# A linear-attention and highway-layer kernel rebuilt as a hand-ordered pipeline, with casting transfers and work on GpSimd

## The chip, the core and the metric

The kernel runs on one core of a Trainium2 chip. A core has TensorE (PE, matrix products into PSUM), VectorE (DVE) and ScalarE (ACT), which read PSUM and SBUF, GpSimd (POOL), which reaches SBUF only, and SyncE (SP), which starts transfers. Sixteen DMA engines carry what SP and POOL start. The metric is the device time of one execution in microseconds (us), the median of some runs; lower is better.

## What is computed

Inputs are q, k, v of shape (4 batches, 8 heads, 768 positions, 64), one decay `lam` per head, and the weights of a highway layer. First comes causal attention without softmax, in which the weight of position j for position i decays as `lam**(i-j)`:

```python
intra = np.einsum('bhic,bhjc->bhij', qb, kb) * Dmask[None]
intra = np.einsum('bhij,bhjd->bhid', intra, vb)
inter = np.einsum('bhid,bhde->bhie', qb * lam_pow[None], kv_state)
out[:, :, sl] = intra + inter
kb_dec = kb * rev_pow[None]
kv_state = lam_block[None, :, None, None] * kv_state + np.einsum('bhsd,bhse->bhde', kb_dec, vb)
```

The heads are then laid side by side, which gives x of 3072 rows and 512 columns, and the layer follows:

```python
H = np.maximum(x @ w_h, 0.0)
T = 1.0 / (1.0 + np.exp(-(x @ w_t + b_t)))
return (T * H + (1.0 - T) * x).astype(np.float32)
```

## The kernel before

The work is cut into 24 chunks: 4 batches (loop at L89) of 6 blocks of 128 positions (loop at L94). A framework places the semaphores, and its scheduler sets each engine's order from the order in which the chunks are written and from what is ready; most tiles have two buffers, PSUM tiles one. Each engine runs its own list in order.

For each chunk SP loads q, k and v for all heads as float32 (`qf`, `kf`, `vf`, L99 to L101, 256 KB each, in pieces of 256 B). DVE multiplies q by `lam**i` (`qs`, L106), v by `lam**-j` (`vb`, L107) and k by `lam**128` (`kb2`, L110; the trace shows it as `kb` too); ACT copies k to bfloat16 (`kb`, L108). PE transposes q and k head by head (L115, L116, 16 products with an identity), and ACT moves the results to SBUF (`qsT` L119, `kbT` L120). Eight products per chunk give the scores (`at_ps`, L132, contraction over 64 rows), and DVE masks them with a triangle in two halves (L133). Then three kinds of product per head: scores by v (L139, contraction over 128 rows, 64 columns), q by the state (L140, contraction over 64 rows, 64 columns) into the same PSUM tile `oa_ps`, and k by v for the next state (`kv2_ps`, L141). DVE copies the attention output to bfloat16 (`x_sbuf`, L143) and updates the state in SBUF with two operations (L145, L146).

The layer needs x transposed: PE does that (L150), ACT moves it (`x_T`, L152), and PE multiplies by the two weights (L156, L162: 4 products each of 512 columns) and adds the bias with a product over one row (L163). ACT applies Relu (L158) and Sigmoid (L165), DVE combines with three operations (L168, L170, L172), and SP stores 256 KB (L174). The weights are loaded as float32 once and cast by ACT (L75 to L79). POOL makes constants at the start and nothing else.

Of the kernel before, what the change touches and what calls it, by code (L numbers as in the profile page):

```python
# [15 lines left out]
def kernel(  # L17
# [24 lines left out]
    tri_mask = singles.tile([128, 1, 128], F32)
    make_upper_triangular(nc, tri_mask[:, 0, :], val=1.0, diag=True)

    lam_bcast = singles.tile([128, H], F32)
    nc.sync.dma_start(out=lam_bcast, in_=lam.partition_broadcast(128))
    ln_lam = singles.tile([128, H], F32)
    nc.scalar.activation(ln_lam, lam_bcast, AF.Ln)
    pow_q = singles.tile([128, H, 1], F32)
    pow_v = singles.tile([128, H, 1], F32)  # L50
    iota_i = work.tile([128, 1], mybir.dt.int32, tag="iota_i")
    nc.gpsimd.iota(iota_i, pattern=[[0, 1]], base=0, channel_multiplier=1)
    iota_f = work.tile([128, 1], F32, tag="iota_f")
    nc.vector.tensor_copy(iota_f, iota_i)
    pln = work.tile([128, H], F32, tag="pln")
    nc.vector.tensor_scalar(pln, in0=ln_lam, scalar1=iota_f, scalar2=None, op0=ALU.mult)
    nc.scalar.activation(pow_q[:, :, 0], pln, AF.Exp)
    nc.vector.reciprocal(pow_v[:, :, 0], pow_q[:, :, 0])
    lam128 = singles.tile([128, H, 1], F32)
    nc.scalar.activation(lam128[:, :, 0], ln_lam, AF.Exp, scale=float(BLK))  # L60
    iota2 = work.tile([128, 128], mybir.dt.int32, tag="iota2")
    nc.gpsimd.iota(iota2, pattern=[[1, 128]], channel_multiplier=0)
    iota2f = work.tile([128, 128], F32, tag="iota2f")
    nc.vector.tensor_copy(iota2f, iota2)
    pln2 = work.tile([128, H, 128], F32, tag="pln2")
    nc.vector.tensor_tensor(pln2, in0=ln_lam[:, :, None].to_broadcast([128, H, 128]),
                            in1=iota2f[:, None, :].to_broadcast([128, H, 128]), op=ALU.mult)
    pow_qT = singles.tile([128, H, 128], F32)
    nc.scalar.activation(pow_qT, pln2, AF.Exp)

    wh = singles.tile([128, KC, d_model], BF16)
    wt = singles.tile([128, KC, d_model], BF16)
    for kc in range(KC):
        tmp = work.tile([128, d_model], F32, tag="wtmp")
        nc.sync.dma_start(out=tmp, in_=moe_w_h[kc * 128:(kc + 1) * 128, :])  # L75
        nc.scalar.activation(wh[:, kc, :], tmp, AF.Copy)
        tmp2 = work.tile([128, d_model], F32, tag="wtmp")
        nc.sync.dma_start(out=tmp2, in_=moe_w_t[kc * 128:(kc + 1) * 128, :])
        nc.scalar.activation(wt[:, kc, :], tmp2, AF.Copy)  # L79
# [125 lines left out]
```

## Time and profile before

| | us |
|---|---|
| median of 3 runs | 248.27 (245.8 to 249.95) |
| span of the profiled execution, first to last instruction | 246.7 |
| PE busy | 209.4 (85%) |
| DVE busy | 155.8 (63%) |
| ACT busy | 111.9 (45%) |
| POOL busy | 1.4 (1%) |
| DMA queue of SP, share of 16 engines | 46.7% |

The profiled execution has no time of its own beside its span; the median of the runs is 1.6 us more than that span. An engine's busy time is the time in which it worked on an instruction; PE's ends are modelled, and matmuls overlap, so the spacing of their starts says more than their length. The chain of work goes back from the last instruction to what released it, step by step. The slices cut the span into 40 equal parts of 6.2 us; PEclk is the granted TensorE clock in tenths of 2.4 GHz, whose two levels are 1.2 and 2.4 GHz.

### The profile page before, as it was taken

The numbers are of one execution on the slowest core, as the hardware profiler recorded it, in microseconds if no ns is written. First come the engines' busy times: TensorE is split into PE (matmuls) and PEld (weight loads), VectorE is DVE, ScalarE is ACT, GpSimd is POOL, SyncE is SP. The second block draws the span as 40 slices with busy tenths as digits, with TensorE's granted clock in tenths as the row PEclk, the third lists the DMA queues.
The fourth block names the chain that finished last, engine by engine and source line by source line (L and its number), as shares of the span: only waits on it lengthen the run. The fifth ranks groups of instructions, "written<-read, shape, count | busy, mean of one in ns | idle before, by whom it ended". The sixth has DMA issues, their size and how long they took to land.

```text
span 246.7 us, 3751 instructions
## 1 busy us (share of the span) xinstructions
PE 209.4 (85%) x1464; PEld 118.4 (48%) x1464; DVE 155.8 (63%) x275; ACT 111.9 (45%) x159; POOL 1.4 (1%) x10
## 2 busy tenths in 40 slices
PE   0158988989898898998998999999979997989972
PEld 0145535455364653645554645645545563654430
DVE  1645675746675767666577667857885775885532
ACT  5664744342634545515544445544543525551210
POOL 2000000000000000000000000000000000000000
PEclk9999979558776987766777769777997576997755
DMA  5699173651754737444453743745355553110111
GB/s 130 198 264 175 45 170 101 115 128 43 170 123 94 170 88 171 115 101 103 110 128 91 166 89 86 169 88 128 86 130 130 141 128 72 43 45 1 43 43 43
DMA packets 79651, 27.51 MB, mean 111 GB/s; under 512 B 75537, under 2 KB 75537, under 8 KB 79634
## 3 DMA queue, kind: packets, MB, share of 16 engines
q1 hardware_dynamic: 79634, 27.28, 46.7%
q8 instruction: 11, 0.18, 0.3%
q14 instruction: 6, 0.05, 0.1%
HBM read 20.98 MB, written 6.29 MB: 111 GB/s over the span
## 4 chain that ended last, share of the span: by engine, by line
PE 76%; ACT 9%; DVE 7%; DMA 4%; issue 2%; SPq 0%; ACTq 0%; DVEq 0%
PE h_ps L156 16%; PE t_ps L162 14%; PE oa_ps L139 10%; PE oa_ps L140 10%; PE qT_ps L115 6%; PE kT_ps L116 5%; PE at_ps L132 5%; DVE x_sbuf L143 5%; ACT x_T L152 4%; PE t_ps L163 4%; PE xps L150 4%; PE kv_ps L141 3%; DMA vf<-in_v_dram 1%; DMA tmp<-in_moe_w_h_dram 1%; ACT kbT L120 1%
## 5 line engine op out<-in xcount | busy, mean ns | idle before, releaser
L156 PE MATMUL h_ps<-wh,x_T 128*128 128x512 bf16 x96 | 40.7, 572 | 4.8 <-ACT x_T L152 4.4
L139 PE MATMUL oa_ps<-vb,masked 128*128 128x64 bf16 x192 | 39.7, 207 | 0.5 <-DVE masked L133 0.4
L140 PE MATMUL oa_ps<-kv,qsT 64*128 64x64 bf16 x192 | 39.1, 204 | 0.0
L133 DVE TENSOR_TENSOR masked<-at_ps,tri_mask 128x512 bf16<-128x512 f32 x48 | 32.8, 683 | 8.9 <-PE at_ps L132 8.7
L162 PE MATMUL t_ps<-wt,x_T 128*128 128x512 bf16 x96 | 38.3, 543 | 0.0
L119 ACT ACTIVATE qsT<-qT_ps 64x1024 bf16<-64x1024 bf16 x24 | 24.4, 1016 | 29.1 <-PE qT_ps L115 22.2
L143 DVE CAST x_sbuf<-oa_ps 128x512 bf16<-128x512 f32 x24 | 16.6, 692 | 28.7 <-PE oa_ps L140 28.7
L115 PE MATMUL qT_ps<-id,qs 128*64 128x128 bf16 x192 | 23.2, 243 | 12.6 <-DVE qs L106 11.6
L158 ACT ACTIVATE h_sb<-h_ps 128x512 bf16<-128x512 f32 x24 | 14.3, 597 | 37.4 <-PE h_ps L156 37.4
L120 ACT ACTIVATE kbT<-kT_ps 64x1024 bf16<-64x1024 bf16 x24 | 24.2, 1010 | 13.0 <-PE kT_ps L116 13.0
L168 DVE TENSOR_TENSOR hmx<-h_sb,x_sbuf 128x512 bf16<-128x512 bf16 x24 | 10.2, 423 | 27.0 <-ACT h_sb L158 26.9
L165 ACT ACTIVATE t_sb<-t_ps 128x512 bf16<-128x512 f32 x24 | 14.3, 597 | 27.2 <-PE t_ps L163 26.1
L116 PE MATMUL kT_ps<-id,kb 128*64 128x128 bf16 x192 | 25.3, 256 | 0.3 <-ACT kb L108 0.3
L115 PEld LDWEIGHTS <-qs 128*64 128x64 bf16 x192 | 18.0, 123 | 14.0 <-DVE qs L106 11.6
L139 PEld LDWEIGHTS <-masked 128*128 128x128 bf16 x192 | 18.5, 97 | 11.5 <-issue 0.7
L162 PEld LDWEIGHTS <-x_T 128*128 128x128 bf16 x96 | 13.1, 137 | 22.7 <-issue 20.1
L132 PE MATMUL at_ps<-qsT,kbT 64*128 64x128 bf16 x192 | 21.6, 238 | 2.2 <-ACT kbT L120 1.3
L140 PEld LDWEIGHTS <-qsT 64*128 64x128 bf16 x192 | 18.0, 94 | 8.2
L152 ACT ACTIVATE x_T<-xps 128x512 bf16<-128x512 bf16 x24 | 14.2, 592 | 16.7 <-PE xps L150 16.7
L116 PEld LDWEIGHTS <-kb 128*64 128x64 bf16 x192 | 19.8, 132 | 1.8 <-ACT kb L108 0.6
L150 PE MATMUL xps<-id,x_sbuf 128*128 128x128 bf16 x96 | 12.3, 268 | 9.0 <-DVE x_sbuf L143 9.0
L145 DVE TENSOR_TENSOR kv2t<-kv,lam 64x512 bf16<-64x512 bf16 x24 | 16.2, 673 | 5.1 <-ACT lam L60 5.1
(41 smaller groups left out, 191.8 us busy)
## 6 DMA issues: line engine op xcount, KB each, us to landing
qf<-in_q_dram SPq DMA_DIRECT2D x24, 256.0 KB, 3.6
kf<-in_k_dram SPq DMA_DIRECT2D x24, 256.0 KB, 3.7
vf<-in_v_dram SPq DMA_DIRECT2D x24, 256.0 KB, 3.4
out_dram<-o_sb SPq DMA_DIRECT2D x24, 256.0 KB, 2.2
tmp<-in_moe_w_h_dram SPq DMA_DIRECT2D x4, 256.0 KB, 3.4
tmp<-in_moe_w_t_dram SPq DMA_DIRECT2D x4, 256.0 KB, 3.2
lam_bcast<-in_lam_dram SPq DMA_DIRECT2D x1, 4.0 KB, 2.9
bt_f<-in_moe_b_t_dram SPq DMA_DIRECT2D x1, 2.0 KB
```

The source lines that it names most:

```text
L115: nc.tensor.transpose(qT_ps[:, h, :], qs[:, h, :], id128)
L116: nc.tensor.transpose(kT_ps[:, h, :], kb[:, h, :], id128)
L119: nc.scalar.activation(qsT, qT_ps, AF.Copy)
L120: nc.scalar.activation(kbT, kT_ps, AF.Copy)
L132: nc.tensor.matmul(at_ps[:, hh, :], lhsT=kbT_h(h), rhs=qsT_h(h), start=True, stop=True)
L133: nc.vector.tensor_tensor(masked[:, g * (H // 2):(g + 1) * (H // 2), :], in0=at_ps, in1=tri_mask.to_broadcast([128, H // 2, BLK]), op=ALU. ...
L139: nc.tensor.matmul(oa_ps[:, h, :], lhsT=masked[:, h, :], rhs=vb[:, h, :], start=True, stop=False)
L140: nc.tensor.matmul(oa_ps[:, h, :], lhsT=qsT_h(h), rhs=kv2_h(h), start=False, stop=True)
L143: nc.vector.tensor_copy(x_sbuf, oa_ps)
L152: nc.scalar.activation(x_T, xps, AF.Copy)
L156: nc.tensor.matmul(h_ps, lhsT=x_T[:, kc, :], rhs=wh[:, kc, :], start=(kc == 0), stop=(kc == KC - 1))
L162: nc.tensor.matmul(t_ps, lhsT=x_T[:, kc, :], rhs=wt[:, kc, :], start=(kc == 0), stop=False)
```

## The change

The kernel is written anew, with the framework's scheduler off (`manual_schedule`), so that each engine's list is the order in the source.

- **Loads.** q and k (L53, L58) and the weights (L98, L99) are loaded by POOL, which casts them to bfloat16 on the way: per batch 8 transfers of 192 KB for q (96 partitions of 8 positions each) and 6 of 256 KB for k. v stays float32 on SP: per chunk in batch 0, else 1.57 MB in one transfer (L64). Batches 0 and 1 are loaded ahead of the loop, batches 2 and 3 at the end of passes 5 and 11.
- **Scaling.** q and k are not scaled. v is scaled by POOL (L165) with powers that run over the whole batch, and the output by `lam**i` where it leaves PSUM (L191).
- **Transposes.** Two heads at a time, 128 columns in one product: 4 for k per chunk (L158), 32 for q per batch (L150), in one shared PSUM tile `tr`.
- **Attention output.** It is made transposed, `o_ps` of 128 rows (two heads) and 4 x 128 columns: 4 products with a block-diagonal state (L184) and 8 with v as the stationary operand (L188). x in rows is made from it by 4 products with an identity (L209).
- **State.** It stays in PSUM and is added to by 4 products per chunk (L200); ACT copies its diagonal blocks to SBUF (L204, two copies).
- **Layer.** Relu and the subtraction are one DVE operation (L216); POOL does the last addition (L230). The bias is a product over 128 rows, of which two hold the bias.
- **Order.** Pass i of the loop does: first half of the layer for chunk i-1, scores for i+1, attention and state for i, second half of the layer for i-1, transpose of k for i+2.

```diff
...
+    ctx.enter_context(tc.manual_schedule())
...
+            nc.gpsimd.dma_start(out=qb[b][:, :, h, :], in_=q[b, h].rearrange("(p j) d -> p j d", j=J))
...
+        nc.gpsimd.dma_start(out=kb[b][:, c], in_=k[b, :, c * C:(c + 1) * C, :].rearrange("h p d -> p h d"))
...
+    nc.gpsimd.dma_start(out=wh, in_=moe_w_h.rearrange("(kc p) n -> p kc n", p=128))
+    nc.gpsimd.dma_start(out=wt, in_=moe_w_t.rearrange("(kc p) n -> p kc n", p=128))
...
-            nc.vector.tensor_tensor(qs, in0=qf, in1=pow_q.to_broadcast([128, H, D]), op=ALU.mult)
-            nc.vector.tensor_tensor(vb, in0=vf, in1=pow_v.to_broadcast([128, H, D]), op=ALU.mult)
-            nc.scalar.activation(kb, kf, AF.Copy)
...
-                nc.tensor.matmul(oa_ps[:, h, :], lhsT=masked[:, h, :], rhs=vb[:, h, :], start=True, stop=False)
-                nc.tensor.matmul(oa_ps[:, h, :], lhsT=qsT_h(h), rhs=kv2_h(h), start=False, stop=True)
...
+        tr = ps.tile([128, J, QP], BF16, tag="tr", name="tr")
+        for j in range(J):
+            nc.tensor.transpose(tr[:, j, :], qb[b][:, j, 2 * hp:2 * hp + 2, :], id128[0:QP, 0:QP])
+        nc.scalar.activation(qT[b][:, hp].rearrange("p c (q j) -> p (c q) j", j=J),
+                             tr.rearrange("p j q -> p q j"), AF.Copy)
...
+        nc.gpsimd.tensor_tensor(vs[n], in0=vf[b][:, :, c, :], in1=pow_k[:, :, c, :].to_broadcast([C, H, D]), op=ALU.mult)
...
+                nc.tensor.matmul(o_ps[n][:, hp, :], lhsT=s_bd[n % 2][:, hp, :], rhs=qT[b][:, hp, c, :],
+                                 start=(hp == 0), stop=False, skip_group_check=True)
...
+                nc.tensor.matmul(o_ps[n][64 * e:64 * e + 64, hp, :], lhsT=vs[n][:, 2 * hp + e, :], rhs=masked[n][:, e, hp, :],
...
+        nc.vector.tensor_tensor(xT[n], in0=o_ps[n], in1=pow_q[:, :, c * C:(c + 1) * C], op=ALU.mult)
...
+            nc.tensor.matmul(kv_ps[b][:, hp, :], lhsT=kb[b][:, c, 2 * hp:2 * hp + 2, :], rhs=vs[n][:, 2 * hp:2 * hp + 2, :],
...
+        nc.vector.scalar_tensor_tensor(hmx[n], in0=h_ps, scalar=0.0, in1=x_sb[n], op0=ALU.max, op1=ALU.subtract)
...
+        nc.gpsimd.tensor_tensor(o_sb, in0=thmx, in1=x_sb[n], op=ALU.add)
...
+    for i in range(N + 1):
+        if i >= 1:
+            ffn_xh(i - 1)
+        if i + 1 < N:
+            scores(i + 1)
+            scale_v(i + 1)
+        if i < N:
+            attn(i)
+            state(i)
+        b, c = divmod(i, NCH)
+        if c < NP and b + 1 < B:
+            trans_q(b + 1, c)
+        if i >= 1:
+            ffn_t(i - 1)
+            combine(i - 1)
+        if i + 2 < N:
+            trans_k(i + 2)
+        if c == NCH - 1 and b + 2 < B:
+            load_v(b + 2)
+            for c in range(NCH):
+                load_k(b + 2, c)
+            load_q(b + 2)
...
```

Three places in the engines' lists. The names in brackets are semaphores: `DMASW0` to `DMASW7` are eight lanes that POOL's transfers take in turn, and a transfer that names a lane waits until the one eight before it has landed. The first place is POOL's list at the start of the program, before, where it makes constants:

```order
masks.py:197 MEMSET id_64 128x128
masks.py:65 MEMSET tri_mask 128x128
masks.py:199 ISA
masks.py:199 AFFINE_SELECT id_64<-id_64 128x128 [waits Pool_49]
masks.py:66 AFFINE_SELECT tri_mask<-tri_mask 128x128 [waits Pool_49]
L52 IOTA iota_i 128x1
L62 IOTA iota_90 128x128
```

And the same place now, without the lanes, where `qb_76`, `kb_74` and `vf_85` belong to batch 0, `qb_118` and `kb_127` to batch 1:

```order
L94 IOTA tq_i 128x768
L58 DMA kb_74<-in_k_dram 128x8x64
L98 DMA wh<-in_moe_w_h_dram 128x4x512
L99 DMA wt<-in_moe_w_t_dram 128x4x512
L58 DMA kb_74<-in_k_dram 128x8x64 x4
L53 DMA qb_118<-in_q_dram 96x8x64 x8
L58 DMA kb_127<-in_k_dram 128x8x64 x6
L165 TENSOR_TENSOR vs<-vf_85,pow_k 128x512 x3
L230 TENSOR_TENSOR o_sb<-thmx,x_sb 128x512
```

The transfers of both batches and of the weights, 30 with the 9 that stand ahead of these rows, come before the first scaling of v. The second place is POOL's list at the end of pass 5, now (before, POOL has nothing there); `kb_661` and `qb_668` belong to batch 2:

```order
L165 TENSOR_TENSOR vs<-vf_134,pow_k 128x512 [waits DMAHW3_49,PE_49,Pool_49]
L230 TENSOR_TENSOR o_sb<-thmx,x_sb 128x512 [waits DMAHW5_49,DVE_49]
L58 DMA kb_661<-in_k_dram 128x8x64 [waits DMASW6_49,PE_49]
L58 DMA kb_661<-in_k_dram 128x8x64 [waits DMASW7_49]
L58 DMA kb_661<-in_k_dram 128x8x64 [waits DMASW0_49]
L58 DMA kb_661<-in_k_dram 128x8x64 [waits DMASW1_49]
L58 DMA kb_661<-in_k_dram 128x8x64 [waits DMASW2_49]
L58 DMA kb_661<-in_k_dram 128x8x64 [waits DMASW3_49]
L53 DMA qb_668<-in_q_dram 96x8x64 [waits DMASW4_49]
L53 DMA qb_668<-in_q_dram 96x8x64 [waits DMASW5_49]
L53 DMA qb_668<-in_q_dram 96x8x64 [waits DMASW6_49]
```

Five more transfers of q follow before the next scaling of v, that of chunk 7. The third place is PE's list in pass 6, now, where the transposes of q for batch 2 begin:

```order
L200 LDWEIGHTS kb_127
L200 MATMUL kv_ps<-vs,kb_127 128x128
L150 LDWEIGHTS qb_668 [waits DMASW5_49,DMASW4_49]
L150 MATMUL tr<-id_91,qb_668 128x96 [waits PE_49]
L150 LDWEIGHTS qb_668
```

They wait for the first two transfers of q, the 7th and 8th of the 14 that POOL starts at the end of pass 5. Before, the same work on PE, the transposes of a chunk's q and k, stands among the products of the chunk ahead, and what it needs comes from DVE and ACT:

```order
L140 LDWEIGHTS qsT
L140 MATMUL oa_ps<-kv_786,qsT 128x64
L141 LDWEIGHTS kb_1236
L141 MATMUL kv_ps<-vb,kb_1236 64x64
L115 LDWEIGHTS qs
L115 MATMUL qT_ps<-id_64,qs 64x128
```

So the loads of a batch, which were spread over its six chunks, now stand in one block, and PE's list meets the transfers themselves.

## Rows read from the trace of the kernel before

**Rows 1.** Page, part 1: busy time, share of the span, instructions.

```profile
PE 209.4 (85%) x1464; PEld 118.4 (48%) x1464; DVE 155.8 (63%) x275; ACT 111.9 (45%) x159; POOL 1.4 (1%) x10
```

**Rows 2.** Page, part 2: 40 slices, busy tenths and granted clock.

```profile
PE   0158988989898898998998999999979997989972
PEclk9999979558776987766777769777997576997755
```

**Rows 3.** Page, part 4: chain that ended last, by engine, then by line.

```profile
PE 76%; ACT 9%; DVE 7%; DMA 4%; issue 2%; SPq 0%; ACTq 0%; DVEq 0%
PE h_ps L156 16%; PE t_ps L162 14%; PE oa_ps L139 10%; PE oa_ps L140 10%; PE qT_ps L115 6%; PE kT_ps L116 5%; PE at_ps L132 5%; DVE x_sbuf L143 5%; ACT x_T L152 4%; PE t_ps L163 4%; PE xps L150 4%; PE kv_ps L141 3%; DMA vf<-in_v_dram 1%; DMA tmp<-in_moe_w_h_dram 1%; ACT kbT L120 1%
```

**Rows 4.** Timeline, PE, 172 to 178 us: start, length, operation, count.

```profile
172.36 0.20 PE L139 MATMUL oa_ps<-vb,masked 128*128 128x64 bf16 x1
172.50 0.20 PE L140 MATMUL oa_ps<-kv,qsT 64*128 64x64 bf16 x1
172.63 0.20 PE L139 MATMUL oa_ps<-vb,masked 128*128 128x64 bf16 x1
...
173.43 0.63 PE L115 MATMUL qT_ps<-id,qs 128*64 128x128 bf16 x8
...
177.08 1.04 PE L156 MATMUL h_ps<-wh,x_T 128*128 128x512 bf16 x4 [0.17 <-ACT x_T L152]
177.96 1.03 PE L162 MATMUL t_ps<-wt,x_T 128*128 128x512 bf16 x4
```

**Rows 5.** Timeline, PE, 159 to 169 us, the same operations at wider spacing.

```profile
159.79 1.89 PE L156 MATMUL h_ps<-wh,x_T 128*128 128x512 bf16 x4
161.47 1.91 PE L162 MATMUL t_ps<-wt,x_T 128*128 128x512 bf16 x4
...
167.02 1.06 PE L116 MATMUL kT_ps<-id,kb 128*64 128x128 bf16 x8
```

**Rows 6.** Windows: us, busy of PE, PEld, DVE, ACT, POOL, granted clock, DMA share, GB/s.

```profile
175.92:184.20 8.28, 6.68 (x59) 4.02 (x59) 7.48 (x14) 3.93 (x7) 0.00 (x0) 0.99 0.40 101
105.00:106.00 1.00, 1.00 (x5) 0.41 (x4) 1.00 (x3) 0.00 (x0) 0.00 (x0) 0.50 0.36 63
```

**Rows 7.** Groups by line: shapes, count; busy, mean ns; idle before.

```profile
L133 DVE TENSOR_TENSOR masked<-at_ps,tri_mask 128x512 bf16<-128x512 f32 x48 | 32.8, 683 | 8.9 <-PE at_ps L132 8.7
L107 DVE TENSOR_TENSOR vb<-vf,pow_v 128x512 bf16<-128x512 f32 x24 | 16.3, 677 | 2.5 <-DMA vf<-in_v_dram 2.5
L170 DVE TENSOR_TENSOR thmx<-t_sb,hmx 128x512 bf16<-128x512 bf16 x24 | 10.1, 422 | 13.0 <-ACT t_sb L165 12.9
L119 ACT ACTIVATE qsT<-qT_ps 64x1024 bf16<-64x1024 bf16 x24 | 24.4, 1016 | 29.1 <-PE qT_ps L115 22.2 <-PE oa_ps L140 5.0 <-PE at_ps L132 1.4
L165 ACT ACTIVATE t_sb<-t_ps 128x512 bf16<-128x512 f32 x24 | 14.3, 597 | 27.2 <-PE t_ps L163 26.1 <-DVE vb L107 1.1
L60 ACT ACTIVATE lam<-ln_lam 128x8 f32<-128x8 f32 x1 | 0.2, 209 | 0.0
masks.py:66 POOL TENSOR_SCALAR_AFFINE_SELECT tri_mask<-tri_mask 128x128 f32<-128x128 f32 x1 | 0.3, 293 | 0.0
```

**Rows 8.** Windows, columns as in rows 6: three stretches with 256 KB loads.

```profile
93.00:94.00 1.00, 0.48 (x6) 0.27 (x6) 0.70 (x2) 1.00 (x2) 0.00 (x0) 1.00 0.94 278
94.00:95.00 1.00, 0.77 (x12) 0.63 (x12) 1.00 (x2) 0.83 (x3) 0.00 (x0) 1.00 1.07 243
95.00:96.00 1.00, 0.91 (x5) 0.40 (x4) 1.00 (x3) 0.59 (x2) 0.00 (x0) 0.68 1.20 251
```

**Rows 9.** Transfers: SP's issues in the timeline, then time to landing.

```profile
11.02 0.43 SPq L101 DMA_DIRECT2D vf<-in_v_dram  x1
15.58 1.88 SPq L99 DMA_DIRECT2D qf<-in_q_dram  x1
...
qf<-in_q_dram SPq DMA_DIRECT2D x24, 256.0 KB, 3.6
out_dram<-o_sb SPq DMA_DIRECT2D x24, 256.0 KB, 2.2
```

More of the change, by code (lines that the diff above doesn't have):

```diff
@@ L40 @@
+    nc.sync.dma_start(out=bt_f[32:33, :], in_=moe_b_t.partition_broadcast(1))
     id128 = singles.tile([128, 128], BF16)
     make_identity(nc, id128)
[L42 to L79, printed above, removed]
@@ new lines, in scores @@
+    def scores(n):
+        b, c = divmod(n, NCH)
+        s_ps = ps.tile([C, 2, NP, C], F32, tag="s", name="s_ps")
+        for hp in range(NP):
+            for e in range(2):
+                r = slice(64 * e, 64 * e + 64)
+                nc.tensor.matmul(s_ps[:, e, hp, :], lhsT=kT[n][r, hp, :], rhs=qT[b][r, hp, c, :], start=True, stop=True)
+        masked[n] = work.tile([C, 2, NP, C], BF16, tag="masked", name="masked")
+        for e in range(2):
+            nc.vector.tensor_tensor(masked[n][:, e], in0=s_ps[:, e],
+                                    in1=tri.to_broadcast([C, NP, C]), op=ALU.mult)
@@ new lines, in state @@
+    def state(n):
+        b, c = divmod(n, NCH)
+        if c == NCH - 1:
+            return
+        if c == 0:
+            kv_ps[b] = ps.tile([128, NP, 128], F32, tag="kv", name="kv_ps")
+        for hp in range(NP):
+            nc.tensor.matmul(kv_ps[b][:, hp, :], lhsT=kb[b][:, c, 2 * hp:2 * hp + 2, :], rhs=vs[n][:, 2 * hp:2 * hp + 2, :],
+                             start=(c == 0 and hp == 0), stop=True, skip_group_check=True)
+        for e in range(2):
+            r = slice(64 * e, 64 * e + 64)
+            nc.scalar.activation(s_bd[(n + 1) % 2][r, :, r], kv_ps[b][r, :, r], AF.Copy)
@@ new lines, in ffn_t, with combine @@
+    def ffn_t(n):
+        t_ps = ps.tile([C, DM], F32, tag="t", name="t_ps")
+        for kc in range(KC):
+            nc.tensor.matmul(t_ps, lhsT=xT[n][:, kc, :], rhs=wt[:, kc, :], start=(kc == 0), stop=False)
+        nc.tensor.matmul(t_ps, lhsT=ones_r, rhs=bt, start=False, stop=True)
+        t_sb[n] = work.tile([C, DM], BF16, tag="t_sb", name="t_sb")
+        nc.scalar.activation(t_sb[n], t_ps, AF.Sigmoid)
+    def combine(n):
+        thmx = work.tile([C, DM], BF16, tag="thmx", name="thmx")
+        D_ENG.tensor_tensor(thmx, in0=t_sb[n], in1=hmx[n], op=ALU.mult)
+        o_sb = work.tile([C, DM], F32, tag="o_sb", name="o_sb", bufs=3)
+        nc.gpsimd.tensor_tensor(o_sb, in0=thmx, in1=x_sb[n], op=ALU.add)
+        nc.sync.dma_start(out=out[n * C:(n + 1) * C, :], in_=o_sb)
```

211 lines of the change are left out of this document (128 added, 83 removed).

## Prediction

> **What bounds the kernel now.** I read the busy times first, then the slices, the chain, PE's timeline, and last the transfers. PE is busy for 209.4 of 246.7 us and DVE for 155.8 [rows 1]; in the slices PE stands at 8 or 9 from the third on [rows 2]. The chain agrees: 76% of it is PE's, spread over all its lines, and only 7% DVE's and 9% ACT's [rows 3]. So a chunk lasts as long as PE needs for it, and PE's time is to be taken apart.
>
> PE's rows have two prices, by the granted clock. At 2.4 GHz (window clock 0.99 [rows 6]) four products of 512 columns are followed by the next four after 0.88 us, 0.22 us each, and eight transposes of 128 columns take 0.63 us, 0.06 us each without the last one's tail [rows 4]. At 1.2 GHz (0.50 in the 105th microsecond [rows 6]) they are 1.68 us apart, 0.42 us each, and eight transposes take 1.06 us, 0.12 us each [rows 5]. Third, at either level the products of L139 and L140, 64 columns each, follow each other every 0.135 us [rows 4], though half as wide as a transpose: they alternate between contractions over 128 and over 64 rows, and each change costs about 0.075 us. A chunk has 16, 2.2 us. The clock falls after such stretches and returns after the 512-column products, and the slices show it wander between 5 and 9 [rows 2].
>
> **The change, part by part.** *PE.* A pass has 32 products of 128 columns (k 4, scores 8, output 12, state 4, x 4), on average 4 transposes of q (96 spread over 24 passes; 96 columns, taken like 128) and 9 of 512 columns. At full clock that is 36 x 0.06 + 9 x 0.22 = 4.1 us, and about four changes of array shape add 0.3; with 0.3 for waits I take 4.7 us. At half clock it is 36 x 0.12 + 9 x 0.42 + 0.6 = 8.7 us.
>
> *The other engines* have less, and the skew lets them work on another chunk than PE. DVE: three operations out of PSUM and the Relu with subtraction, 0.68 each by L133, one at 0.42 (L170): 3.1 us. ACT: four moves of 0.6 (L165 is 0.60; two of them, the state's copies of 256 elements, lie between L60's 0.21 and 0.60, I take 0.4), and two thirds of a 768-element move (between 0.60 and L119's 1.02): about 3.1 us. POOL: two operations of 512 elements; the trace has none, but the triangle's select of 128 takes 0.293 us, four times that is 1.17 and DVE's 0.68 the lower bound: 2.3 us [rows 7]. All are covered by PE's 4.7 us; without cover the longest, DVE, would end a pass at 3.1 us and change nothing.
>
> *The loads ahead of the loop.* POOL must start 30 transfers before the first scaling of v, and the 30th waits until the 22nd has landed. These 22 carry 6.62 MB of float32 (6 x 0.262 of k, 15 x 0.197 of q, 2.10 of weights); SP's 3.15 MB of v for both batches share the engines. Three windows full of such loads moved 278, 243 and 251 GB/s at shares of 0.94, 1.07 and 1.20 [rows 8]: 240 GB/s for a full share. So 9.77 MB take 40.7 us; 3 us more for the start and the landing (a 256 KB load lands after 3.6 us [rows 9], 1.1 of them moving) and 1.17 for the scaling: the first attention begins at 44.9 us. PE, DVE and ACT have almost nothing to do until then. That assumes that a cast transfer moves like a plain one: for its time I know two bounds, by the bytes written (half) and twice the time per piece, and take the plain row, which reads as many bytes in as many pieces.
>
> *What POOL pays to start one.* No row has it. SP's issue of the same shape takes 0.43 us and at most 1.88 [rows 9]; POOL does it in software, and piece by piece at the select's 2.3 ns per element [rows 7] 1024 pieces make 2.35 us. I take about 1.2: anything below 1.4 hides under the moving bytes above.
>
> The Trainium skill (DMA: Bandwidth & Descriptors, Anatomy of one DMA — SWDGE (gpsimd) path) says of descriptor generation: "You can emit a lot of descriptors before the incremental cost shows up". By that rule the charge is small and the sum stays at 212; at 2.35 us each it would be 266. No run here shows it yet.
>
> *The loads in the loop.* At the end of passes 5 and 11 POOL starts 14 transfers, and PE's transposes of q in the next pass wait for the 7th and 8th. In front of them lie 1.97 MB of k and q, 1.57 MB of v, which SP starts at that time, and about 0.5 MB of stores: 4.04 MB, 16.8 us, with landing about 18.7. POOL begins 2.2 us after PE's last product of pass 5 (0.60 + 0.42 + 1.17); PE needs 2.9 us to reach the transposes. So PE stands for 18.7 - 0.7 = 18 us, twice. Behind PE's wait stand the second half of the layer, and with it ACT, DVE and the stores. Behind the transfers on POOL stand the next scaling of v and the addition; at 1.2 us each 14 of them take 17 us, which ends with PE's wait.
>
> *Clock.* The alternating stretch is gone, and a pass is dense in columns, so I expect full clock in most passes, and half in one behind each long stop (the start, and twice): 21 x 4.7 + 3 x 8.7 = 124.8, less 2.2 for pass 0, which has no layer: 122.6 us. The last chunk's layer follows: 2.3 on PE, 0.60, 0.42, 1.17 and 2.2 for the store [rows 7, 9], 6.7 us.
>
> *Sum:* 44.9 + 122.6 + 2 x 18 + 6.7 = 210.2 us of span against 246.7. The median of the runs is 1.6 above the span; with it 211.8, so **212 us**.
>
> **The rivals.** *A, POOL's starts are the bound (slower).* At g us per transfer the start takes 30 g + 4.2, and a boundary is set by the scaling of v for chunk 7, behind 14 starts: 14 g + 1.2, less the 3.9 us in which PE would get there, twice. The total is 58 g + 129.7. It passes my sum at g = 1.42, the time before at 2.04, and gives 266 at 2.35. For it speaks that each transfer has 768 or 1024 pieces, against it SP's 0.43 for the same.
>
> *B, the clock stays at half.* Then 24 x 8.7 - 4 + 44.9 + 2 x 16 + 8.5 + 1.6 = 292. Against it: rows at half clock come here behind the alternating products, of which none is left; for it, the long stops.
>
> *C, cast transfers are slower per piece.* They write 128 B where now 256 B are written. At twice the time the 6.62 MB count as 13.24: 68.3 us, first attention at 72.5; boundaries (3.94 + 1.57 + 0.5) / 240 = 25 us, stops of 26.3. Total 72.5 + 122.6 + 52.6 + 8.3 = 256. The Trainium skill (DMA: Bandwidth & Descriptors, Specifications) has a rule for it: pieces under 512 B are below line rate, since the engine reads, modifies and writes. By that rule before's 256 B pieces would suffer as well, and its windows moved 240 GB/s, so the trace doesn't bear it out fully.
>
> *D, better throughout.* Full clock in every pass: 24 x 4.7 - 2.2 = 110.6, total 200. If casts also move by bytes written, the start falls to 31.1 and a stop to 14: 178.
>
> **How the numbers follow.** My forecast 0.48 (own range 200 to 226, by a pass of 4.3 to 5.3), A 0.14, B 0.08, C 0.13, D 0.17. The time is the likeliest's, 212. The range 180 to 252 leaves out B, the half of A above g = 2.1, a little of C, and less than D's lower end, together 0.2. Faster by over 2% (below 243.3): forecast, D, half of C (up to about 1.7 times the time) and 0.04 of A: 0.76. Within 2% (about what a measurement can tell from no change): 0.06. Slower: 0.18.
>
> **What would show it.** In the new profile the first `vs` of POOL should start near 43 us, with the DMA share near 1 until then; if POOL's starts follow each other without a wait for DMA there, A holds. PE should stand for about 18 us, released by a transfer of q, near a third and two thirds of the span. In between, x to x should be 4.5 to 5 us at a clock near 1; 8 us and 0.5 mean B. DVE near 77 us, ACT near 75. Wrong is the forecast if the loads ahead end before 30 or after 60 us, or if passes take over 5.5 us at full clock, since then a wait that I hide (the shared `tr` tile, the single PSUM tiles) stands on the path.

## The result and the profile after

The changed kernel takes 198.47 us (median of 4 runs, 197.84 to 199.19) against 247.19 for the kernel before, run beside it: a ratio of 0.804, interval 0.798 to 0.809. The forecast was 212, in a range of 180 to 252.

The page of the changed kernel first: busy time of each engine, then four of the rows of 40 slices (4.9 us each), then the chain that ended last by engine and by line.

```profile
PE 105.8 (54%) x1080; PEld 61.0 (31%) x1080; DVE 74.3 (38%) x132; ACT 74.7 (38%) x142; POOL 101.8 (52%) x116
...
PE   0013420000797999000499999100299999999980
...
POOL 7585531189304456943644445961835444655442
PEclk9999999999999999955589999955579999999999
DMA  0899999999501111999931111799962211112112
...
issue 41%; DMA 30%; POOL 27%; POOLq 1%
DMA kb<-in_k_dram 24%; POOL vs L165 13%; DMA qb<-in_q_dram 6%; POOL qb L53 6%; POOL o_sb L230 4%; POOL kb L58 4%; POOLq L292 1%; POOLq L165 0%; POOLq L230 0%; POOLq L58 0%; POOLq L281 0%
```

PE is busy for half of what it was [rows 1], and the slices are no longer an even row [rows 2]: three stretches of 7 to 9, and ahead of each a stretch of zeros in which DMA stands at 9. The chain, 76% PE before [rows 3], has no PE in it. So the time is now three waits for loads and three blocks of work between them, and each is read from its own rows.

**The first wait.** POOL's timeline (start, length, instruction, and in brackets the idle time before it with what ended it), then the first product of the attention on PE:

```profile
39.60 1.67 POOL L53 DMA_DIRECT2D qb<-in_q_dram  x2 [0.37 <-DMA kb<-in_k_dram]
...
42.25 5.29 POOL L58 DMA_DIRECT2D kb<-in_k_dram  x6
47.48 3.16 POOL L165 TENSOR_TENSOR vs<-vf,pow_k 128x512 bf16<-128x512 f32 x3
...
48.68 0.64 PE L188 MATMUL o_ps<-masked,vs 128*64 128x128 bf16 x8 [20.70 <-POOL vs L165]
```

POOL waits for earlier transfers until 39.6 us, then makes the last nine of its 30 starts almost without a wait and scales v at 47.48. PE, which has been ready for 20.7 us, begins the attention at 48.68.

**The stops.** PE's and POOL's timeline at the end of the sixth pass:

```profile
95.99 0.80 PE L150 MATMUL tr<-id,qb 96*128 96x96 bf16 x8 [17.64 <-DMA qb<-in_q_dram]
...
77.90 5.32 POOL L58 DMA_DIRECT2D kb<-in_k_dram  x6
...
91.43 3.06 POOL L53 DMA_DIRECT2D qb<-in_q_dram  x4 [5.14 <-DMA kb<-in_k_dram]
...
95.53 1.07 POOL L165 TENSOR_TENSOR vs<-vf,pow_k 128x512 bf16<-128x512 f32 x1
```

PE waits 17.64 us for a transfer of q, and 17.74 the second time. Almost at the same moment, at 95.53, POOL comes through its 14 starts to the scaling of v for the next chunk: two waits that end 0.6 us apart (95.99, and 95.53 + 1.07). Of POOL's 17.6 us from 77.90 to 95.53 its 14 starts take 11.5; the other 6.2, most of it the 5.14 ahead of 91.43, are waits for earlier transfers to land.

**The passes.** One pass without transposes of q, at a granted clock of 1.00:

```profile
113.19 0.39 PE L209 MATMUL x_ps<-id,xT 128*128 128x128 bf16 x4
113.41 1.03 PE L214 MATMUL h_ps<-wh,xT 128*128 128x512 bf16 x4
114.37 0.40 PE L173 MATMUL s_ps<-qT,kT 64*128 64x128 bf16 x8
114.70 0.40 PE L184 MATMUL o_ps<-qT,s_bd 128*128 128x128 bf16 x4
115.02 0.41 PE L188 MATMUL o_ps<-masked,vs 128*64 128x128 bf16 x8
115.37 0.40 PE L200 MATMUL kv_ps<-vs,kb 128*128 128x128 bf16 x4
115.60 1.03 PE L221 MATMUL t_ps<-wt,xT 128*128 128x512 bf16 x4
116.47 0.38 PE L222 MATMUL t_ps<-bt,ones_r 128*128 128x512 bf16 x1
116.68 0.39 PE L158 MATMUL tr<-id,kb 128*128 128x128 bf16 x4
117.10 0.40 PE L209 MATMUL x_ps<-id,xT 128*128 128x128 bf16 x4
```

From x to x it is 3.91 us. With the eight transposes of q it is 4.57 (108.62 to 113.19). The spacing of the starts prices each group: four products of 512 columns 0.87, four of 128 columns over the whole array 0.22 to 0.23, eight that use half of the array (the scores, L173, and the products by v, L188) 0.33 to 0.35. Just ahead of either half-array group the spacing is 0.09 to 0.10 longer: 0.96 from `h_ps` to the scores instead of 0.87, and 0.32 from L184 to L188 instead of 0.23.

**POOL's prices**, from the groups by line (count; busy, mean ns; idle before):

```profile
L230 POOL TENSOR_TENSOR o_sb<-thmx,x_sb 128x512 f32<-128x512 bf16 x24 | 27.7, 1153 | 57.9 <-DVE thmx L228 57.9
L53 POOL DMA_DIRECT2D qb<-in_q_dram x32 | 24.7, 775 | 29.2 <-DMA kb<-in_k_dram 21.9
L165 POOL TENSOR_TENSOR vs<-vf,pow_k 128x512 bf16<-128x512 f32 x24 | 25.4, 1068 | 0.0
L58 POOL DMA_DIRECT2D kb<-in_k_dram x24 | 21.7, 926 | 3.3 <-DMA qb<-in_q_dram 2.5
```

A start takes 0.78 us for 768 pieces and 0.93 for 1024, an operation of 512 elements 1.07 or 1.15.

### The profile page after: what moved, and what is told of

The parts are those of the page before. It is cut to its first block, busy times and chain, and to the rows that moved or that the text cites. A ratio compares the mean times of both kernels' runs of the same rounds, so it can differ in the third digit from the quotient of the medians.

```text
span 196.0 us, 2858 instructions
## 1 busy us (share of the span) xinstructions
PE 105.8 (54%) x1080; PEld 61.0 (31%) x1080; DVE 74.3 (38%) x132; ACT 74.7 (38%) x142; POOL 101.8 (52%) x116
## 3 DMA queue, kind: packets, MB, share of 16 engines
q0 software_dynamic: 51104, 7.34, 59.7%
## 4 chain that ended last, share of the span: by engine, by line
issue 41%; DMA 30%; POOL 27%; POOLq 1%
DMA kb<-in_k_dram 24%; POOL vs L165 13%; DMA qb<-in_q_dram 6%; POOL qb L53 6%; POOL o_sb L230 4%; POOL kb L58 4%; POOLq L292 1%; POOLq L165 0%; POOLq L230 0%; POOLq L58 0%; POOLq L281 0%
## 5 line engine op out<-in xcount | busy, mean ns | idle before, releaser
L230 POOL TENSOR_TENSOR o_sb<-thmx,x_sb 128x512 f32<-128x512 bf16 x24 | 27.7, 1153 | 57.9 <-DVE thmx L228 57.9
L53 POOL DMA_DIRECT2D qb<-in_q_dram x32 | 24.7, 775 | 29.2 <-DMA kb<-in_k_dram 21.9
L176 DVE TENSOR_TENSOR masked<-s_ps,tri 128x512 bf16<-128x512 f32 x48 | 30.7, 681 | 9.7 <-PE s_ps L173 9.7
L204 ACT ACTIVATE s_bd<-kv_ps 64x256 bf16<-64x256 f32 x40 | 15.1, 378 | 49.8 <-PE kv_ps L200 49.4
L150 PE MATMUL tr<-id,qb 96*128 96x96 bf16 x128 | 10.2, 237 | 42.9 <-DMA qb<-in_q_dram 38.6
L221 PE MATMUL t_ps<-wt,xT 128*128 128x512 bf16 x96 | 26.5, 400 | 0.0
L214 PE MATMUL h_ps<-wh,xT 128*128 128x512 bf16 x96 | 25.7, 392 | 0.0
L165 POOL TENSOR_TENSOR vs<-vf,pow_k 128x512 bf16<-128x512 f32 x24 | 25.4, 1068 | 0.0
L191 DVE TENSOR_TENSOR xT<-o_ps,pow_q 128x512 bf16<-128x512 f32 x24 | 16.4, 682 | 20.1 <-PE o_ps L188 20.1
L58 POOL DMA_DIRECT2D kb<-in_k_dram x24 | 21.7, 926 | 3.3 <-DMA qb<-in_q_dram 2.5
L216 DVE SCALAR_TENSOR_TENSOR hmx<-h_ps,x_sb 128x512 bf16<-128x512 f32 x24 | 16.6, 692 | 17.9 <-ACT x_sb L211 9.3
L150 PEld LDWEIGHTS <-qb 96*128 96x128 bf16 x128 | 8.2, 115 | 43.8 <-DMA qb<-in_q_dram 37.8
L188 PE MATMUL o_ps<-masked,vs 128*64 128x128 bf16 x192 | 10.3, 231 | 20.7 <-POOL vs L165 20.7
L224 ACT ACTIVATE t_sb<-t_ps 128x512 bf16<-128x512 f32 x24 | 14.3, 595 | 14.0 <-PE t_ps L222 14.0
L158 PE MATMUL tr<-id,kb 128*128 128x128 bf16 x96 | 10.3, 236 | 16.3 <-POOL id masks.py:199 11.8
L158 PEld LDWEIGHTS <-kb 128*128 128x128 bf16 x96 | 8.0, 106 | 23.6 <-DMA kb<-in_k_dram 10.9
L211 ACT ACTIVATE x_sb<-x_ps 128x512 bf16<-128x512 f32 x24 | 14.3, 597 | 0.1
L188 PEld LDWEIGHTS <-vs 128*64 128x64 bf16 x192 | 6.3, 113 | 23.4 <-POOL vs L165 21.0
L173 PE MATMUL s_ps<-qT,kT 64*128 64x128 bf16 x192 | 10.4, 229 | 3.3 <-ACT kT L160 2.9
## 6 DMA issues: line engine op xcount, KB each, us to landing
vf<-in_v_dram SPq DMA_DIRECT2D x6, 256.0 KB, 10.8
```

Source lines behind the costliest of these rows:

```text
L53: nc.gpsimd.dma_start(out=qb[b][:, :, h, :], in_=q[b, h].rearrange("(p j) d -> p j d", j=J))
L58: nc.gpsimd.dma_start(out=kb[b][:, c], in_=k[b, :, c * C:(c + 1) * C, :].rearrange("h p d -> p h d"))
L150: nc.tensor.transpose(tr[:, j, :], qb[b][:, j, 2 * hp:2 * hp + 2, :], id128[0:QP, 0:QP])
L158: nc.tensor.transpose(tr[:, hp, :], kb[b][:, c, 2 * hp:2 * hp + 2, :], id128)
L165: nc.gpsimd.tensor_tensor(vs[n], in0=vf[b][:, :, c, :], in1=pow_k[:, :, c, :].to_broadcast([C, H, D]), op=ALU.mult)
L176: nc.vector.tensor_tensor(masked[n][:, e], in0=s_ps[:, e], in1=tri.to_broadcast([C, NP, C]), op=ALU.mult)
```

## Experiments

The reading so far says: the time is the first wait, two stops made by the blocks of loads, and passes that PE sets. Each part was changed by itself, with what its edit needed beside it. All times are medians of 4 runs; the stretches come from each run's own trace. What the rewrite saved on PE itself (105.8 us busy instead of 209.4) no run takes apart.

### Where the loads stand

**Loads of batches 2 and 3 pass by pass.** The tiles of k and v hold one chunk here, and v of batch 1 comes in six transfers instead of one. The part of the edit that moves the loads:

```diff
-        if c == NCH - 1 and b + 2 < B:
-            load_v(b + 2)
-            for c in range(NCH):
-                load_k(b + 2, c)
-            load_q(b + 2)
+        if i < N and b + 2 < B:
+            load_v(b + 2, c)
+            load_k(b + 2, c)
+            load_q(b + 2, [(0, 1), (2, 3), (4,), (5,), (6,), (7,)][c])
```

> Only the place of the loads of batches 2 and 3 changes: instead of 14 GpSimd transfers and one of v in a block at the end of passes 5 and 11, each pass of batches 0 and 1 starts one of k, one of v and one or two of q (k and v now have tiles of one chunk, in the same SBUF). Theory: the two stops of PE (17.64 and 17.74 us, released by a transfer of q) come from the block alone; they vanish, and nothing takes their place: 198 - 35 = 163 us. GpSimd then needs 1.07 + 1.15 + 0.93 + 0.78 or 1.56 = 3.9 or 4.7 us per pass, so four passes may grow by 0.8: up to 166. Rival 1: the bytes bound it, six passes of 4 us against 4 x 1.57 MB per batch (q, k, v and the stores) at 240 GB/s = 26 us: 163 + 2 x 2 = 167 or more, with waits for DMA spread over the passes. Rival 2: GpSimd's starts wait for earlier transfers in the middle of passes and hold up the scaling of v: passes of 5 to 6 us in batches 0 and 1, 175 to 185.

Measured: 162.76 us (ratio to the kernel before 0.657, 0.654 to 0.660), 35.7 us less than the changed kernel; the two stops were 35.4. PE's longest wait (total us, times, longest):

```profile
PE o_ps L183 <- POOL vs L160: 22.2, 1, 22.2
```

The first wait is left; of the waits for q only two short ones of the start (3.2 us). From the third pass to the last but one all lie between 3.9 and 4.6 us, those with loads among them. So the stops came from the block, and neither bytes nor POOL took their place. That gain and stops agree to 0.3 us is chance: the passes at half clock behind the stops went too, 2.0 us (below), and the first attention came 2.4 us later, at 51.05. Why it did no run here tells; the smaller transfers of v are one candidate.

**A short start.** The 14 transfers of batch 1 leave the list ahead of the loop.

```diff
-    load_q(1)
-    for c in range(NCH):
-        load_k(1, c)
...
+        if i < NCH:
+            load_q(1, [(0, 1, 2, 3), (4, 5, 6, 7), (), (), (), ()][i])
+            load_k(1, i)
...
-        if c < NP and b + 1 < B:
-            trans_q(b + 1, c)
+        if 1 <= c <= NP and b + 1 < B:
+            trans_q(b + 1, c - 1)
```

> Only the start changes: the 14 GpSimd transfers of batch 1 leave the list ahead of the first scaling of v and are started in passes 0 to 5 (q in passes 0 and 1, one k per pass; the transposes of q for batch 1 move by one pass, to passes 1 to 4). The blocks for batches 2 and 3 stay. Theory: the first attention, now at 48.7 us, waits for 30 starts of which the last eight wait for lanes; with 16 starts it comes at about 20 to 25 us, but the layer of chunk 0 then waits for the weights, which have 4.2 MB of casting transfers and some of v before them, about 30 us. Gain 15 to 20 us: 180 to 184 us. Rival: what holds the start is the rate of the DMA engines for all 9.77 MB, and it only moves into the passes of batch 0, which then wait for q and k of batch 1: gain under 8 us, 190 to 198.

Measured: 184.06 us (0.743, 0.740 to 0.746), 14.4 less than the changed kernel, just under the 15 to 20 expected. The first attention begins at 28.59 us, but PE then stands 9.4 us for the transfer of k of chunk 2, which was not expected, and the first layer begins at 39.57 instead of 51.94, 12.4 earlier. The two stops together are 5.2 us shorter, and some 3.5 us are given back in the passes of batch 0 and behind the stops. PE now has its stops at another place; the first of them:

```profile
87.27 0.64 PE L186 MATMUL o_ps<-masked,vs 128*64 128x128 bf16 x8 [15.73 <-POOL vs L163]
```

As the transposes of q come a pass later here, no transfer holds PE; POOL does, with the scaling of v behind its 14 starts. It costs 15.7 and, the second time, 14.5 us instead of 17.6 and 17.7. That is the place where rival A looked, and it lay hidden behind the transfer of q. But it is not POOL's starts alone: in the first block of this run, too, POOL waits 5.7 us for transfers to land (the last run of the next section shows the block without such waits).

**Both**, the loads of batches 2 and 3 two passes later than above.

```diff
+        if i >= 2 and i - 2 < 2 * NCH:
+            bl, cl = divmod(i - 2, NCH)
+            load_v(bl + 2, cl)
+            load_k(bl + 2, cl)
...
```

> Both changes together: only batch 0 and the weights are loaded ahead of the first scaling, and batches 1 to 3 are started pass by pass (batch 2 and 3 two passes later than they would be free, so that batch 1 goes first). Theory: the gains add, since one lies ahead of the loop and one in it: 198 - 35 - 17 = 146 us. Rival: with the start and the stops gone the bytes bound it: 12 loads of 1.57 MB, 2.1 MB of weights and 6.3 MB of stores are 27.3 MB, 114 us at 240 GB/s, which is below 146, but in batches 0 and 1 two batches' loads fall into few passes; waits for DMA then give back 10 to 20 us: 156 to 166.

Measured: 154.47 us (0.624, 0.621 to 0.626), between the two expectations: the two gains, 35.7 and 14.4, would give 148.4. From its waits of PE:

```profile
PE tr L142 <- DMA qb<-in_q_dram: 9.1, 3, 5.8
...
PE o_ps L180 <- POOL vs L157: 4.9, 6, 1.5
```

Some is given back as waits for q of batch 1, some as waits for scaled v: with two starts of q and one of k, POOL's part of a pass is 2.22 + 1.55 + 0.93 = 4.7 us, more than PE's.

### What ends a stop

**q first in the block.**

```diff
         if c == NCH - 1 and b + 2 < B:
+            load_q(b + 2)
             load_v(b + 2)
             for c in range(NCH):
                 load_k(b + 2, c)
-            load_q(b + 2)
```

> One line moves: in the blocks at the end of passes 5 and 11 the eight transfers of q come before v and the six of k. My prediction took PE's stop from the bytes ahead of the 7th and 8th transfer. Theory from the new trace: the scaling of v for the next chunk stands on GpSimd behind all 14 starts (it ran at 95.5, PE's stop ended at 96.0), so PE passes the transposes early, does about 3 to 5 us of work more and then stops for the scaled v instead: gain 2 x 3 to 4 us, 190 to 193 us, with PE's stop now released by POOL at L188 and no longer by DMA at L150. Rival: only q's transfers hold PE, which then come 1st and 2nd and land after some 5 to 7 us: gain 2 x 11 us, 176 us.

Measured: 189.3 us (0.763, 0.759 to 0.768). Both were partly wrong. PE has two waits in each stop; the first stop (the second has 9.63 and 2.83):

```profile
88.41 0.80 PE L150 MATMUL tr<-id,qb 96*128 96x96 bf16 x8 [10.17 <-DMA qb<-in_q_dram]
96.45 0.64 PE L188 MATMUL o_ps<-masked,vs 128*64 128x128 bf16 x8 [2.56 <-POOL vs L165]
```

Even the first two of the 14 transfers make PE stand for 10 us. They are not served before the others: what is in flight shares the engines, and SP's transfer of v starts almost with them, so being first in POOL's list buys 7.5 us, not 11 or 12. And the scaled v comes next, as expected.

**The same, with v scaled two passes ahead.**

```diff
...
-            scale_v(i + 1)
+        if i + 2 < N:
+            scale_v(i + 2)
```

> As e4_qfirst (q first in the blocks), and v is scaled two passes ahead instead of one (four buffers), so that the next chunk's scaled v lies ready before GpSimd starts a block. In e4_qfirst PE stood 10.2 and 9.6 us for the first two transfers of q and then 2.6 and 2.8 us for the scaled v. Theory: the two waits are separate; the second goes and the first stays: 189.3 - 5.4 = 184 us. Rival: the wait for v only covered the layer of the chunk behind it, which then waits for GpSimd's addition or a store: 187 to 189.

Measured: 184.21 us (0.743, 0.738 to 0.749). The waits for scaled v are gone from the stops, those for q are 10.19 and 9.60, and 5.1 us are saved of the 2.56 + 2.83 that PE stood for v. The two waits are separate.

**v taken out of the block** (order as in the changed kernel, a third buffer for v):

```diff
+        if c == 2 and b + 2 < B:
+            load_v(b + 2)
         if c == NCH - 1 and b + 2 < B:
-            load_v(b + 2)
```

> Only v's 1.57 MB leave the blocks: they are loaded at the end of passes 2 and 8, into a third buffer. My prediction counted them into the 4.04 MB that lie ahead of PE in a stop, at a rate that the two queues share. Theory: the share holds, 6.5 us less traffic per block; GpSimd's 14 starts of 0.78 to 0.93 us and one scaling (13 us) then become the longer way: stops of 12 to 13 us, 198 - 10 = 188 us. Rival: the casting queue has a rate of its own, which v does not slow: stops stay at 17.7 and the time at 198.

Measured: 184.16 us (0.744, 0.737 to 0.752). The first stop (the second has 10.06):

```profile
88.71 0.80 PE L150 MATMUL tr<-id,qb 96*128 96x96 bf16 x8 [9.92 <-DMA qb<-in_q_dram]
```

POOL's timeline in the same block, and k's six transfers of the block (KB written, median us from issue to landing), in the changed kernel and then here:

```profile
78.33 5.32 POOL L58 DMA_DIRECT2D kb<-in_k_dram  x6
83.60 6.13 POOL L53 DMA_DIRECT2D qb<-in_q_dram  x8
...
kb<-in_k_dram POOLq DMA_DIRECT2D x6, 128.0 KB, 12.0
...
kb<-in_k_dram POOLq DMA_DIRECT2D x6, 128.0 KB, 4.1
```

1.57 MB less make a stop 7.7 us shorter (204 GB/s), and each transfer lands after 4 us instead of 12. So bytes of the two queues do count together, as the prediction's sum had it. POOL no longer waits between its starts: the block takes it 11.4 us instead of 17.6, and PE doesn't stand for the scaled v. So 204 GB/s is an estimate of the shared rate and not the rate itself, since what is left of the stop is made of POOL's first eight starts (78.33 to about 85.2) and a landing. The 12 to 13 us that I expected from POOL's starts were too many: PE reaches the transposes behind the eighth transfer, not behind the last start. This also bears on the run with q first, where v was in flight beside the two transfers that PE waited for; q first with v taken out was not run.

### Does the cast cost

**The same transfers without a cast.**

```diff
-            qb[b] = load.tile([QP, J, H, D], BF16, tag="qb", name=f"qb{b}")
+            qb[b] = load.tile([QP, J, H, D], F32, tag="qb", name=f"qb{b}")
...
+    def top(ap):
+        return ap.bitcast(BF16)[..., 1::2]
```

> GpSimd's transfers of q, k and the weights no longer cast: they move float32 to float32 by the same queue, in as many pieces of 256 B, and PE reads the high half of each value as bfloat16 (so values are cut, not rounded). All else as in the changed kernel. My prediction took a casting transfer like a plain one. Theory: that holds, so the first attention stays near 48.7 us, the stops near 17.7 us, and the time near 198 us (195 to 202). Rival C: the cast makes each piece slower (36.6 ns a packet in flight after, 23.1 before), then plain transfers cut the start by 10 to 13 us and a stop by 5 to 6: 174 to 178 us. Rival D: the bytes written count, which double: start 13 us longer, stops 4 to 6 longer: 220 or more.

Measured: 199.11 us (0.800, 0.792 to 0.808), as the changed kernel. First attention and first stop, the row of POOL's queue (packets, MB, share), and v's first six transfers on SP (KB, median us to landing), in the changed kernel and then here:

```profile
43.41 0.64 PE L192 MATMUL o_ps<-masked,vs 128*64 128x128 bf16 x8 [15.98 <-POOL vs L169]
92.91 0.80 PE L154 MATMUL tr<-id,qb 96*128 96x96 bf16 x8 [19.60 <-DMA qb<-in_q_dram]
...
q0 software_dynamic: 4512, 14.68, 34.7%
...
vf<-in_v_dram SPq DMA_DIRECT2D x6, 256.0 KB, 10.8
...
vf<-in_v_dram SPq DMA_DIRECT2D x6, 256.0 KB, 27.6
```

The first attention comes 5.3 us earlier, the stops are 2.0 and 1.6 us longer, passes a few hundredths longer, the second pass behind a stop by 0.7 and 1.1 us. In sum nothing. That a transfer with the cast is slower is not shown: the start is shorter without it, but there v's transfers on SP land after 27.6 us instead of 10.8, so POOL's queue went ahead at v's cost, and in the stops PE waits longer. The factor of two of rival C shows nowhere. Why the queues share otherwise without the cast, no run here tells.

**Half of the bytes in as many pieces.** As the run without the cast, but only the first half of each piece of q, of k and of each weight row is loaded; the other half holds ones, so the kernel leaves out half of these inputs.

```diff
-        nc.gpsimd.dma_start(out=kb[b][:, c], in_=k[b, :, c * C:(c + 1) * C, :].rearrange("h p d -> p h d"))
+        nc.gpsimd.dma_start(out=kb[b][:, c, :, 0:D // 2], in_=k[b, :, c * C:(c + 1) * C, :].rearrange("h p d -> p h d")[:, :, 0:D // 2])
```

> As the run without the cast, but only the first half of each piece of q, k and each weight row is moved (float32, 128 B per piece for q and k, 1 KB for weights), in as many pieces; the other half holds ones, so half of the inputs is left out. Theory: the bytes read set the time of the start and of the stops; with half of them GpSimd's 30 starts of 0.78 to 0.93 us and v's 3.15 MB remain: first attention near 30 us, stops near 13 us (14 starts), 198 - 18 - 9 = 171 us. Rival: the number of pieces sets it; then start and stops stay as without the cast, near 198 us.

Measured: 177.76 us (0.716, 0.710 to 0.721).

```profile
33.80 0.64 PE L199 MATMUL o_ps<-masked,vs 128*64 128x128 bf16 x8 [9.51 <-POOL vs L176]
...
78.17 0.80 PE L161 MATMUL tr<-id,qS 96*128 96x96 bf16 x8 [14.49 <-DMA qS<-in_q_dram]
```

Against the run without the cast the first attention moves from 43.4 to 33.8, a stop from 19.5 to 14.3. So bytes count, and not pieces alone. It didn't reach 171, since a stop kept 14 us where I had expected 13 and the start 34 where I had expected 30.

### What sets a pass

**The gate's products made twice.**

```diff
+        for kc in range(KC):
+            nc.tensor.matmul(t_ps, lhsT=xT[n][:, kc, :], rhs=wt[:, kc, :], start=False, stop=False)
```

> The four products of 512 columns by the gate's weights are made twice per chunk (so the gate's argument counts them twice); nothing else changes. Theory: in a pass PE has no slack, a pass of 3.92 or 4.57 us is its columns plus some tenths, so each of 24 chunks costs four products more, 0.88 us: 21 us, less what falls into the two stops: 217 to 220 us. Rival: a pass is set by the chain through DVE, ACT and GpSimd, and PE waits in it: then up to half of that is hidden, 205 to 210.

Measured: 212.8 us (0.854, 0.847 to 0.862), 14.3 more, between theory and rival. In a pass with transposes of q:

```profile
113.33 0.38 PE L224 MATMUL t_ps<-bt,ones_r 128*128 128x512 bf16 x1
113.54 0.39 PE L158 MATMUL tr<-id,kb 128*128 128x128 bf16 x4
113.77 0.39 PE L209 MATMUL x_ps<-id,xT 128*128 128x128 bf16 x4
```

Here PE goes from bias (113.33) to k's transposes in 0.21 us and to x in another 0.23: it stands nowhere. x to x is 4.93, so PE's own time in the kernel without the doubling is 4.93 - 0.87 = 4.06 us, and of its 4.57 us 0.5 are waits, which the added products fill. Without transposes of q it is 4.58 - 0.87 = 3.71 against 3.92. The waits have names: in PE's rows the transposes of k wait until ACT has copied q's out of the shared tile `tr`, and x waits for `xT`, which DVE makes behind both masks.

### A version from these readings

**Loads in order of need**, two or three a pass ahead of POOL's addition, v in four buffers, two transfers of q of batch 1 ahead of the loop. A line or two of its table:

```diff
+        3: [('k', 1, 0), ('k', 1, 1)],
+        4: [('k', 1, 2), ('q', 2, 0), ('q', 2, 1)],
...
+        for x, bl, a in PLAN.get(i, ()):
+            load_q(bl, (a,)) if x == "q" else load_k(bl, a)
```

> A version built from the runs so far: as e3_both, but v is held back to four chunks in flight (four buffers), only two transfers of q for batch 1 are started ahead of the loop, and the other 40 follow in the order of need, two or three per pass, ahead of the addition on GpSimd. In e3_both the first layer began at 35.2 us, the second 12.9 us later, and passes with loads took 4.4 to 5.5 us, held by the scaling of v on GpSimd. Theory: v's 3.1 MB no longer compete with q and the weights, so the first layer begins near 28 us, the gap behind it closes, and GpSimd has 2.22 + 2.33 x 0.85 = 4.2 us per pass, inside PE's mean of 4.35: 28 + 23 x 4.2 + 8 + 1.6 = 134 to 140 us. Rival: GpSimd still ends last, since a start needs longer when lanes are waited for: passes of 4.7 to 5 us up to the 17th: 146 to 150.

Measured: 140.74 us (0.566, 0.562 to 0.570), just above the theory's 134 to 140. From the third pass to the last but one all are 4.5 to 4.6 or 3.9 us, so POOL no longer shows on PE. The first layer begins at 31.15 rather than 28, and the one behind it 6.7 us later, not 12.9.

**PE in another order**: attention and transposes of q ahead of the next scores, the state behind them.

```diff
-            scores(i + 1)
             scale_v(i + 1)
...
             attn(i)
-            state(i)
...
             trans_q(b + 1, c - 1)
+        if i + 1 < N:
+            scores(i + 1)
+        if i < N:
+            state(i)
```

> As e9_order, but PE makes the attention of chunk i and the transposes of q before the scores of chunk i+1, and the state after them. Doubling the gate's products showed PE's own time in a pass: 4.93 - 0.87 = 4.06 us with transposes of q, 4.58 - 0.87 = 3.71 without; the rest of 4.57 and 3.92 are waits, for the copy of q's transposes out of the shared tile tr (about 0.5) and for the output of the attention, which DVE makes behind both masks (about 0.2). Theory: both leave: 12 x 0.5 + 11 x 0.2 = 8 us at most, but GpSimd has 4.2 us a pass up to the 17th, so about half comes: 136 to 137 us. Rival: another wait on DVE takes their place, since the mask then ends later: 140 us, no change.

Measured: 136.39 us (0.552, 0.548 to 0.556; 136.31 to 137.59 against 140.51 to 140.80). At the end of a pass with transposes PE goes from the bias (73.18) to k's transposes (73.40) and to x (73.62) in 0.22 us each: the waits are gone, and x to x is 4.06 us, the number that the doubling had given. About half of the possible 8 us came: the first pass is 2.7 us longer (9.4), and waits for scaled v (2.3 us) and for q (5.2 us, 3.6 before) show in their place. It is the fastest version of this study.

## Why the prediction was right, and where its numbers were off

The mechanism was right: PE's passes, the long wait ahead of them, two stops. The sum was 13 us too high, and not evenly:

| term | forecast | measured | from |
|---|---|---|---|
| first attention | 44.9 | 48.7 | row at 48.68 |
| 24 passes | 122.6 | 104.2 | 188.23 (x of chunk 23) - 48.68 - 35.38 |
| two stops | 36.0 | 35.4 | 17.64 + 17.74 |
| last layer | 6.7 | 7.8 | 196.0 - 188.23 |
| median over span | 1.6 | 2.5 | 198.47 - 196.0 |
| sum | 211.8 | 198.5 | |

- **The clock** was the first mis-sized step: three whole passes at half clock, 12 us. Windows of the changed kernel (columns as in [rows 6]) around the first stop:

```profile
86.00:96.00 10.00, 0.01 (x1) 0.04 (x2) 0.00 (x0) 0.00 (x0) 4.60 (x7) 0.50 2.38 163
...
98.00:100.00 2.00, 2.00 (x13) 1.18 (x12) 0.35 (x1) 1.04 (x3) 0.00 (x0) 0.51 0.55 26
100.00:102.00 2.00, 2.00 (x29) 1.16 (x28) 1.18 (x3) 0.54 (x2) 1.84 (x2) 1.00 0.00 0
```

  The granted clock is 0.50 while PE stands and for some 4 us behind, but it returns within the pass: the passes behind the three waits cost 1.6, 0.85 and 0.85 us over 4.57, and the next one 0.3 behind the first stop; 3.6 us in all. Pass 0, right behind the first wait, is not in this count; it ran at the spacing of half clock too (3.26 us from 48.68 to 51.94). Rival B, 292 us, needed the half clock to stay. Not priced at all was ACT's table load (1.28 us, at 57.83); it stands ahead of the gate of the pass from 58.08 to 63.65, which is a microsecond longer than its like.
- **The price of a pass** was the second: 4.7 us, measured 4.57 with and 3.92 without transposes of q. The columns were right where they were 512 wide. Too high were the eight scores and the eight products by v, which use half of the array, taken at 0.06 each. Inside the pass shown above they start in pairs (the view is taken from 114.36 to 114.42 and from 114.72 to 114.75, so it counts only what runs then):

```profile
114.06 0.38 PE L214 MATMUL h_ps<-wh,xT 128*128 128x512 bf16 x1
114.37 0.23 PE L173 MATMUL s_ps<-qT,kT 64*128 64x128 bf16 x2
...
114.55 0.22 PE L173 MATMUL s_ps<-qT,kT 64*128 64x128 bf16 x2
```

  Four pairs start between 114.37 and 114.55, 0.06 apart, and each pair takes what one product of 128 columns over the whole array takes. So the sixteen cost about 0.5 us and not 0.96. The 0.3 for four changes of array shape was a little low: the last product of `h_ps` starts at 114.06 and the scores 0.31 behind it, where 0.22 is the spacing of such products; from the last pair of scores to L184 it is 0.15 (114.55 to 114.70), where 0.06 is the spacing of pairs; with the same before and behind L188 four changes cost 0.09 to 0.10 each, 0.38 us. That is near the 0.075 that the prediction read from before [rows 4]. Where it says that these products of before stand 0.135 apart "at either level" of the clock, rows 4 show the upper level only; at a granted clock of 0.50 the trace of before has them 0.167 apart (51.56 to 52.56). The sum doesn't rest on that. The 0.3 for waits was near: 0.5 and 0.2.
- **The start** was 3.8 us too low, though its bytes were priced well: the 22nd transfer landed at 44.5 (39.60, and 4.9 from issue to landing), where the sum had 43.7. POOL's starts cost 0.78 and 0.93 us, below the 1.2 that I took and well below the 1.42 from which they would have set the sum, so A's bound on the total fell; but after the last wait for a transfer nine starts still had to be made, 8 us (39.60 to 47.48), where the forecast had one.
- **The stops** were right to 0.4 us, partly by luck. That bytes of both queues count together is shown (7.7 us for v's 1.57 MB). That bytes ahead in the list decide is not: the first two transfers in it hold PE for 10 us. And POOL's list holds PE almost as long: 17 us at 1.2 us a start, as the sum had it beside the 18, and measured 17.6, but made of 11.5 us of starts and 6.2 us of waits for transfers to land. Without v's bytes in the block it takes 11.4 us and holds PE not at all. So two waits of nearly the same length lay over each other, and the same transfers stretch both.
- **The other engines** came as forecast: DVE 74.3 us busy (77), ACT 74.7 (75), POOL's two operations 2.22 (2.3). In the passes they are covered, but not in all of their order: `tr` and `xT` are the waits of 0.5 and 0.2.
- **Rival A** (POOL's starts) was thus refuted in its price, and right in its place: the nine last starts end the first wait, and the scaling of v behind the block is next in line at a stop. The Trainium skill (DMA: Bandwidth & Descriptors, Anatomy of one DMA — SWDGE (gpsimd) path) says that many descriptors can be emitted before their incremental cost shows. The rows agree: 256 pieces more add 0.15 us to 0.78.
- **Rival C** (casts slower per piece): not in the sum, 199.1 without casts against 198.5. The start is 5.3 us shorter without casts, but v's transfers pay for it. The Trainium skill (DMA: Bandwidth & Descriptors, Specifications) puts pieces under 512 B below line rate. No doubling for 128 B against 256 B shows in these runs.
- **Rival D**, 200 us by full clock throughout, is the case that came nearest, though by another way: part of the half clock stayed, and the cheaper pass made up for it. Its second half, casts that move by the bytes written, is not borne out: twice the bytes written cost nothing in the sum.

## What to carry to other kernels

Loads that are issued by an engine which also computes stand in that engine's list; spread them over the passes in the order of need, since a block of them holds up what waits for the bytes, and also what stands behind the block in that list. When two waits end within a microsecond of each other, taking one away pays only what lies between them: look at what is ready next, and whether the same bytes stretch both, before pricing the gain. To find the slack of a busy engine, give it more work: what the pass does not lengthen by was a wait.
